# A gated attention/FFN decode step on one core: a wider row pitch for the heads' loads, a slice of w_gate by eight small transfers, and x and the gate vectors as rows

## The chip, the cores and the metric

The kernel runs on one core of a Trainium2 chip. The metric is the device time of one execution in microseconds (us); lower is better. The time before is 806.35 us, the median of three runs (806.04 to 806.44). A separate execution was profiled. Its page and its trace are what is read below.

The engines have these names in the profile: PE is the matrix engine (PEld its weight loads), DVE the vector engine, ACT the scalar engine, POOL the general-purpose engine, SP the engine that only issues transfers and waits. Transfers (DMAs) issued by SP or ACT are carried out by 16 DMA engines, which the profile sums up as one row.

## The reference

One token goes through two branches, which are mixed by a gate:

```python
g = sigmoid((x * gate_w).sum(-1))              # one number
a = attention(x) @ wo                          # 32 query heads, 4 kv heads, 65536 cached keys, head size 128
b = x + sigmoid(x @ w_r) * ((silu(x @ w_gate) * (x @ w_up)) @ w_down)   # d = 1024, f = 3584
out = g * a + (1 - g) * b                      # 1024 numbers
```

Everything is float32. With a single token the router's top-1 choice is that token, so the routing is the identity and only its sigmoid stays. The key and value caches have 4 x 65536 x 128 numbers each, 268 MB together; wq and wo are 33.6 MB, and the three FFN weights 44 MB. Each of these bytes is used once.

## The kernel before

**One stream of large loads.** All weights and caches were laid out anew on the host, so that the kernel reads them in one order. For each kv head `g` (G = 4) there are UNITS = 18 units of 32 KiB per partition: one of wq, eight of keys, eight of values, one of wo. Two units make one load, so a head has PER = 9 loads, and the array `heads` has 36 loads of 128 rows; a row is 2*CH = 16384 floats, 64 KiB, and goes to one partition. The rows of `heads` lie back to back. After them comes `ffn`, six loads of TAIL = 14336 floats (56 KiB) per partition: two for w_gate, two for w_up and two for w_down. The last two are cut into two and six pieces by `ENDS`, so that the last piece is small.

**Three buffers.** SP alone issues these loads (lines 114 to 127). Load `i` goes to buffer `i % 3`. From the fourth on, SP first waits for the mark of PE that frees the buffer (`LAST`, line 46): the mark that ends the second unit of the load three before. Two loads are thus issued or under way while PE works on a third.

**The work on a head.** PE forms q from x and wq (line 301), the scores per chunk of 8192 keys (line 317), and, after softmax, the values' sum (line 329) and the product with wo (line 346). ACT copies scores from PSUM and takes exponentials; DVE takes maxima and transposes. Only the gate values and q need x in other layouts: `xp` (line 93) is the stationary matrix for all products with x; column 0 of each of its eight 32-column blocks holds x, the other columns are zero.

**x and the gate vectors.** ACT issues two transfers at the start. `xk <- vecs` (line 149) brings x, gate_w and w_r as 128 rows of 96 bytes: partition p gets elements 8p to 8p+7 of each. `x_row <- x` (line 151) brings x once more, 256 floats to each of partitions 0, 32, 64 and 96. DVE copies xk into `xp` and forms the two dot products (lines 196 to 200). PE adds them up over the partitions (line 292), and q of head 0 follows. `x_row`, scaled by 1 - g, is the residual that is added at the end (lines 209, 269, 271).

**The FFN.** Line 373 multiplies x with w_gate and w_up: for each of eight row blocks `k` there are two banks `e` times four column groups `j` of FN = 448 columns, accumulated in PSUM. Group j writes partitions 32j to 32j+31. After `gate 1` ACT and DVE form the gated hidden vector, which is transposed on DVE and multiplied with w_down (lines 383 and 400). The last DVE instruction writes `fin` (line 271), and SP sends its rows 0, 32, 64, 96 to the output (line 129).

The order on each engine is the order of the lines; no scheduler moves anything. Engines wait for each other by semaphores: `marked` counts PE's marks, `ld0` to `ld2` and `end0` to `end7` the loads.

Of the kernel before, what the change touches and what calls it, by code (L numbers as in the profile page):

```python
# [8 lines left out]
P = 128  # L9
D = 1024  # L10
G = 4
HG = 8
DH = 128
SK = 65536
F = 3584
CH = 8192
# [3 lines left out]
KB = D // P  # L20
NQ = D // 4
FB = F // P
FN = F // 8
# [4 lines left out]
PER = UNITS // 2  # L28
BUFS = 3

TAIL = 14336
NTAIL = 3 * KB * F // TAIL

ENDS = {NTAIL - 2: [8 * D, TAIL], NTAIL - 1: [6 * D, 10 * D, 12 * D, 13 * D, 13 * D + 768, TAIL]}

PIECES = [(0, 192), (192, NQ)]

EARLY = 20

# [9 lines left out]
ACTED = {m: i + 1 for i, m in enumerate(ACTS)}  # L49


def gated_mix_kernel(nc, x, vecs, heads, ffn, out):

# [16 lines left out]
    pe, act, dve, pool, sp = nc.tensor, nc.scalar, nc.vector, nc.gpsimd, nc.sync  # L72

    stream = [nc.alloc_sbuf_tensor(f"st{b}", [P, 2 * CH], F32, align_bytes=256)[:, :] for b in range(BUFS)]
    scores = nc.alloc_sbuf_tensor("s", [P, NCH, 512], F32)[:, :, :]
# [3 lines left out]
    hp = scores[:, 2:4, :].rearrange("p a n -> p (a n)")[:, : FB * 32]  # L79
    att_sb = scores[:, 4, :]  # L80
    zeros = scores[:, 5, :]
    o_sb = scores[:, 0, :].rearrange("p (s d) -> p s d", s=4)

    def sb(name, *shape):
        t = nc.alloc_sbuf_tensor(name, [P, *shape], F32)
        return t[tuple(slice(None) for _ in range(len(shape) + 1))]

    xk = sb("xk", 3, KB)
    x_row, fin, q_sb = sb("x_row", NQ), sb("fin", NQ), sb("q_sb", 2 * NQ)
    ident, ones, md, lb = sb("ident", P), sb("ones", P), sb("md", P), sb("lb", P)  # L90
    sel, sel8, nsel, sel4 = sb("sel", 32), sb("sel8", HG), sb("nsel", HG), sb("sel4", 4)
    half, halves = sb("half", 2), sb("halves", 2, 32)
    xp, qp, op = sb("xp", KB, 32), sb("qp", 4, 32), sb("op", HG, 32)
# [3 lines left out]
    gate = sig[:, 0:1]  # L97
# [5 lines left out]
    ps_s = [ps_u[:, i, :] for i in range(2)]  # L103
    acc, ps_m, att, y = psum("acc", 512), psum("ps_m", P), psum("att", 512), psum("y", NQ)

    names = ["done", "fed", "x1", "x2", "acted", "pooled", "marked", "d2p", "d2a", "d2s", "self"]
    names += [f"ld{b}" for b in range(BUFS)] + [f"end{i}" for i in range(sum(map(len, ENDS.values())))]
    sems = {n: nc.alloc_semaphore(n) for n in names}
    nums = sorted(s.num for s in sems.values())
# [4 lines left out]
    for i in range(G * PER + NTAIL):  # L114
        b = i % BUFS
        if i >= BUFS:
            g, l = divmod(i - BUFS, PER)
            sp.wait_ge(sems["marked"], MARK[f"{LAST[l]} {g}" if g < G else ["gate 0", "gate 1", "up 0"][l]])
        if i < G * PER:
            sp.dma_start(stream[b], heads[i]).then_inc(sems[f"ld{b}"], 16)  # L120
        elif i - G * PER not in ENDS:
            sp.dma_start(stream[b][:, :TAIL], ffn[i - G * PER]).then_inc(sems[f"ld{b}"], 16)
        else:
            cuts = ENDS[i - G * PER]
            for c0, c1 in zip([0] + cuts, cuts):
                sp.dma_start(stream[b][:, c0:c1], ffn[i - G * PER, :, c0:c1]).then_inc(sems[f"end{len(ends)}"], 16)  # L126
                ends.append((i, c0, c1))
# [11 lines left out]
        out=ident, in_=ident, compare_op=ALU.not_equal, fill=1.0, base=0, pattern=[[-1, P]], channel_multiplier=1  # L139
# [3 lines left out]
    acted = []  # L143

    def tell(ins, name):
        acted.append(name)
        return ins.then_inc(sems["acted"])

    act.dma_start(xk, vecs).then_inc(sems["x1"], 16)
    act.wait_ge(sems["d2a"], 1)  # L150
    act.dma_start(
        x_row[::32, :], x.rearrange("(j n) -> j n", j=4)
    ).then_inc(sems["x2"], 16)
    act.wait_ge(sems["marked"], MARK["dot"])
    tell(act.activation(sig, ps_m[:, :2], AF.Exp, scale=-1.0), "sig")
    for g in range(G):
# [4 lines left out]
        for c in range(NCH):  # L161
            t = scores[:, c, :]
# [10 lines left out]
    def then(ins):  # L173

        own[0] += 1
        ins.then_inc(sems["self"])
        dve.wait_ge(sems["self"], own[0])
# [14 lines left out]
    dve.memset(qp, 0.0)  # L192
    dve.memset(zeros, 0.0)
    dve.memset(halves, 0.0)
    then(dve.memset(op, 0.0))
    dve.wait_ge(sems["x1"], 16)
    dve.tensor_copy(xp[:, :, 0], xk[:, 0, :])
    dve.tensor_mul(dots[:, 0, :], xk[:, 0, :], xk[:, 1, :])
    then(dve.tensor_mul(dots[:, 1, :], xk[:, 0, :], xk[:, 2, :]))
    to_pe(dve.tensor_reduce(dsum, dots, AX.X, ALU.add))  # L200
# [4 lines left out]

    then(dve.tensor_scalar(rest[:, 0:1], gate, -1.0, 1.0, op0=ALU.mult, op1=ALU.add))
    then(dve.tensor_mul(rest[:, 1:2], rest[:, 0:1], sig[:, 1:2]))
    dve.wait_ge(sems["x2"], 16)
    dve.tensor_scalar_mul(x_row, x_row, rest[:, 0:1])

    dve.wait_ge(sems["pooled"], 2)
# [64 lines left out]
    def mark(ins, name):  # L276
        marks.append(name)
        ins.then_inc(sems["marked"])

    def take(name, n=1):  # L280
        pe.wait_ge(sems[name], n).then_inc(sems[name], -n)  # L281
# [14 lines left out]
    with pe.Fori(0, G):  # L296
        loaded(0)
        for k in range(KB):
            for f in range(2):
                j = 2 * (k % 2) + f  # L300
# [23 lines left out]
        for c in range(NCH):  # L324
            loaded(1 + NCH + c)
            take("d2p")
            for m in range(NM):
                j = m % 4
# [3 lines left out]
                    stop=(c == NCH - 1 and m >= NM - 4),  # L332
# [10 lines left out]
        for h in range(HG):  # L343
            for f in range(2):
                j = 2 * (h % 2) + f
# [9 lines left out]
    def tail(first, n):  # L355
        i, c = divmod(first, TAIL)
        assert c + n <= TAIL
        if i < min(ENDS):
            if c == 0:
                take(f"ld{(G * PER + i) % BUFS}", 16)  # L360
        else:
            for e, (i1, c0, _) in enumerate(ends):
                if (i1 - G * PER, c0) == (i, c):
                    pe.wait_ge(sems[f"end{e}"], 16)
        return stream[(G * PER + i) % BUFS][:, c : c + n]


    for i, part in enumerate(("gate", "up")):
        ps = (ps_f, ps_u)[i]
        for k in range(KB):  # L370
            for e in range(2):
                for j in range(4):
                    ins = pe.matmul(  # L373
                        ps[32 * j : 32 * j + 32, e, :FN], xp[:, k, :], tail((i * KB + k) * F + (2 * j + e) * FN, FN),
                        start=(k == 0), stop=(k == KB - 1),
                    )
            if k % 4 == 3:
                mark(ins, f"{part} {k // 4}")
    take("d2p")
    for b in range(EARLY):  # L380
        for f in range(2):
            j = 2 * (b % 2) + f
            ins = pe.matmul(  # L383
                att[32 * j : 32 * j + 32, :], hp[:, 32 * b : 32 * b + 32], tail(2 * KB * F + b * D + f * 512, 512),
                start=(b < 2), stop=(b >= EARLY - 2),
            )
    mark(ins, "early")
    for b in range(EARLY, FB):
        if b == EARLY + 4:
            take("d2p")  # L390
            for j in range(4):
                ins = pe.matmul(
                    acc[32 * j : 32 * j + 32, :NQ], halves[:, j // 2, :], att_sb[:, j % 2 * NQ : (j % 2 + 1) * NQ],
                    start=True, stop=True,
                )
            mark(ins, "both")
        for c0, c1 in PIECES if b == FB - 1 else [(0, NQ)]:
            n = c1 - c0
            for j in range(4):
                ins = pe.matmul(  # L400
                    y[32 * j : 32 * j + 32, c0:c1], hp[:, 32 * b : 32 * b + 32], tail(2 * KB * F + b * D + 4 * c0 + j * n, n),
                    start=(b == EARLY), stop=(b == FB - 1 and c1 == NQ),
# [34 lines left out]
```

## Time and profile before

| what | value |
|---|---|
| median of three runs | 806.35 us (806.04 to 806.44) |
| profiled execution | 806.2 us |
| its span, first to last instruction | 804.8 us |
| PE busy | 399.5 us (50%) |
| DVE busy | 75.2 us (9%) |
| ACT busy | 44.5 us (6%) |
| bytes read | 346.05 MB, 430 GB/s over the span |
| granted PE clock | 0.758 |

The page shows the span in 40 slices with the busy share of each engine in tenths, and a row for the 16 DMA engines together. A table of DMA queues gives for each queue its packets, its megabytes and the time of its packets as a share of 16 engines' span: q1 is what SP issues, q10 what ACT issues, and q8 and q14 are fetches of instructions. The chain that ended last is followed back from the last instruction. The timeline lists instructions in order of time, with the idle time before each group in brackets. As PE starts on a load when it has landed, PE's starts in the timeline date the landings. A DMA query for a stretch of time gives the same queue table for that stretch alone; a packet counts in the stretch in which it starts, so shares of a short stretch can exceed 100%.

### The profile page before, as it was taken

How to read it: one execution, taken by the hardware profiler on the slowest of the kernel's cores; microseconds unless marked ns; L12 is line 12 of the kernel's file. 1: busy time of each engine (PE TensorE's matmuls, PEld its weight loads, DVE VectorE, ACT ScalarE, POOL GpSimd, SP SyncE). 2: the span in 40 equal slices, each digit the busy share in tenths (PEclk: the TensorE clock that was granted, in tenths of full speed). 3: DMA queues.
4: the chain of work that ended last, by engine and by line, in shares of the span. 5: the costliest groups of instructions: out<-in, count | busy, mean ns of one | idle time of the engine just before them, and what ended most of it. 6: DMA issues, size and time to landing. Idle time of an engine off the chain costs nothing. (4 is left out here: it accounts for less than half of the span.)

```text
span 804.8 us, 6104 instructions
## 1 busy us (share of the span) xinstructions
PE 399.5 (50%) x2810; PEld 119.5 (15%) x2810; DVE 75.2 (9%) x155; ACT 44.5 (6%) x99; POOL 0.7 (0%) x6
## 2 busy tenths in 40 slices
PE   0544463457554463445544454445444644564465
PEld 0211111112111121111111111111111111121121
DVE  0200010000000020000100110000000100000310
ACT  0000030000000030000000200000000300000000
POOL 0000000000000000000000000000000000000000
PEclk9976767767777786778777687687677677697679
DMA  9999999999999999999999999999999999999997
GB/s 417 417 418 466 414 423 460 417 428 453 420 430 453 420 430 450 423 430 450 423 430 446 427 430 446 427 431 443 427 433 443 427 433 443 421 442 428 436 416 335
DMA packets 7082, 346.20 MB, mean 430 GB/s; under 512 B 920, under 2 KB 1056, under 8 KB 1312
## 3 DMA queue, kind: packets, MB, share of 16 engines
q1 hardware_dynamic: 6920, 346.04, 99.4%
q8 instruction: 8, 0.13, 0.1%
q10 hardware_dynamic: 152, 0.02, 0.0%
q14 instruction: 2, 0.02, 0.0%
HBM read 346.05 MB, written 0.00 MB: 430 GB/s over the span
## 5 line engine op out<-in xcount | busy, mean ns | idle before, releaser
L317 PE MATMUL ps_u<-st,qp 128*32 128x512 f32 x1024 | 148.8, 743 | 154.7 <-PEq L281 154.7
L329 PE MATMUL acc<-st,pt 128*32 128x512 f32 x1024 | 149.9, 747 | 146.5 <-PEq L281 146.5
L317 PEld LDWEIGHTS ps_u<-st,qp 128*32 128x32 f32 x1024 | 40.8, 133 | 259.2 <-issue 259.2
L329 PEld LDWEIGHTS acc<-st,pt 128*32 128x32 f32 x1024 | 41.3, 133 | 251.9 <-issue 251.9
L159 ACT ACTIVATE s<-ps_u 128x512 f32<-128x512 f32 x32 | 19.1, 597 | 561.6 <-PE ps_u L317 561.6
L231 DVE TENSOR_REDUCE mx<-s 128x1 f32<-128x512 f32 x32 | 21.9, 686 | 285.3 <-ACT s L159 285.3
L246 DVE STREAM_TRANSPOSE pt<-s 128x512 f32<-128x512 f32 x32 | 22.7, 711 | 199.6 <-PE acc L329 196.1
L301 PE MATMUL ps_u<-st,xp 128*32 128x512 f32 x128 | 21.6, 835 | 19.8 <-PEq L281 19.8
L373 PE MATMUL ps_u<-st,xp 128*32 128x448 f32 x128 | 16.4, 678 | 17.5 <-PEq L281 17.5
L164 ACT ACTIVATE s<-s,nb 128x512 f32<-128x512 f32 x32 | 22.6, 708 | 10.5 <-DVE nb L241 10.5
L373 PE MATMUL ps_f<-st,xp 128*32 128x448 f32 x128 | 16.0, 664 | 14.1 <-PEq L281 14.1
L346 PE MATMUL att<-st,op 128*32 128x512 f32 x128 | 16.3, 653 | 2.4 <-PEq L281 2.4
L383 PE MATMUL att<-st,s 128*32 128x512 f32 x80 | 12.6, 782 | 7.8 <-DMA st<-in_ffn 5.3
L292 PE MATMUL ps_m<-dsum,ones 128*128 128x2 f32 x2 | 0.6, 348 | 23.6 <-PEq L281 23.6
L301 PEld LDWEIGHTS ps_u<-st,xp 128*32 128x32 f32 x128 | 5.7, 148 | 36.2 <-issue 36.2
L373 PEld LDWEIGHTS ps_u<-st,xp 128*32 128x32 f32 x128 | 5.2, 135 | 28.7 <-issue 28.7
L250 DVE COPY s<-acc 128x512 f32<-128x512 f32 x4 | 2.8, 691 | 70.0 <-PE acc L329 70.0
L373 PEld LDWEIGHTS ps_f<-st,xp 128*32 128x32 f32 x128 | 5.5, 131 | 24.7 <-issue 24.7
L221 DVE COPY q_sb<-ps_u 128x512 f32<-128x512 f32 x4 | 2.8, 691 | 51.6 <-PE ps_u L301 51.6
L167 ACT ACTIVATE s<-ps_f 128x896 f32<-128x896 f32 x1 | 0.9, 917 | 103.7 <-PE ps_f L373 103.7
L346 PEld LDWEIGHTS att<-st,op 128*32 128x32 f32 x128 | 4.9, 118 | 10.4 <-issue 10.4
L323 PE MATMUL ps_m<-md,ones 128*128 128x128 f32 x8 | 2.0, 328 | 8.2 <-PEq L281 8.2
(65 smaller groups left out, 66.9 us busy)
## 6 DMA issues: line engine op xcount, KB each, us to landing
st<-in_ffn SPq DMA_DIRECT2D x4, 7168.0 KB, 42.8
st<-in_ffn SPq DMA_DIRECT2D x2, 3072.0 KB, 37.5
st<-in_ffn SPq DMA_DIRECT2D x1, 4096.0 KB, 35.2
st<-in_ffn SPq DMA_DIRECT2D x1, 2048.0 KB, 37.2
st<-in_ffn SPq DMA_DIRECT2D x1, 1024.0 KB, 39.2
st<-in_heads SPq DMA_DIRECT2D x36, 48.1
st<-in_ffn SPq DMA_DIRECT2D x1, 512.0 KB, 40.0
st<-in_ffn SPq DMA_DIRECT2D x1, 384.0 KB, 40.5
```

Source lines behind the costliest of these rows:

```text
L159: tell(act.activation(scores[:, c, :], ps_s[c % 2], AF.Copy), f"s{c} {g}")
L164: act.activation(t, t, AF.Exp, bias=nb, scale=SCALE, accum_out=sums[:, c : c + 1]), f"e{c} {g}"
L221: to_pe(dve.tensor_copy(q_sb, ps_s[0]))
L231: ins = dve.tensor_reduce(mx[:, c : c + 1], scores[:, c, :], AX.X, ALU.max)
L246: to_pe(dve.transpose(pts[:, c % 2, :], scores[:, c, :]))
L250: to_pe(dve.tensor_copy(o_sb, acc.rearrange("p (s d) -> p s d", s=4)))
L301: ins = pe.matmul(ps_s[0][32 * j : 32 * j + 32, :], xp[:, k, :], unit(0)[:, k * D + f * 512 : k * D + (f + 1) * 512], start=(k < 2), stop= ...
L317: ins = pe.matmul(ps_s[c % 2][32 * j : 32 * j + 32, :], qp[:, s, :], unit(1 + c)[:, (4 * s + j) * 512 : (4 * s + j + 1) * 512], start=(s = ...
L329: ins = pe.matmul(acc[32 * j : 32 * j + 32, :], pts[:, c % 2, 32 * m : 32 * m + 32], unit(1 + NCH + c)[:, m * 512 : (m + 1) * 512], start= ...
L346: ins = pe.matmul(att[32 * j : 32 * j + 32, :], op[:, h, :], unit(UNITS - 1)[:, h * D + f * 512 : h * D + (f + 1) * 512], start=False, sto ...
L373: ins = pe.matmul(ps[32 * j : 32 * j + 32, e, :FN], xp[:, k, :], tail((i * KB + k) * F + (2 * j + e) * FN, FN), start=(k == 0), stop=(k == ...
L383: ins = pe.matmul(att[32 * j : 32 * j + 32, :], hp[:, 32 * b : 32 * b + 32], tail(2 * KB * F + b * D + f * 512, 512), start=(b < 2), stop= ...
```

## The change

The change has three parts.

- **Pitch.** In memory, the rows of `heads` are now PITCH = 17408 floats (68 KiB) apart in place of 64 KiB. A load still brings the first 64 KiB of each row, and the 4 KiB behind it are never read.
- **Side.** The last 256 of the columns of w_gate in row block k = 3 no longer come with the first load of `ffn`, whose rows are 1 KiB shorter on all 128 partitions. They come as an array `side` of 32 rows of 4 KiB, to partitions 0 to 31, by eight transfers of four rows each. SP issues one of them after each of loads 0, 3, 6 up to 21. PE multiplies them by four matmuls of 32 rows and 256 columns, with x from `xside` in `xs`, after row block 4 of the gate; the matmul that read these columns before is narrower by 256.
- **x as rows.** x, gate_w and w_r come as 12 rows of 1 KiB, by three transfers of four rows, into partitions i, 32+i, 64+i, 96+i of `x_row`. A DVE transpose makes `xk` of it. A fourth transfer, `xside`, brings the part of x that goes with `side` (32 rows of 16 bytes). All four are issued by ACT, after DVE has cleared `x_row`. DVE waits once for all of them. The order of x over partitions and blocks has changed with this, and so has the host's layout of wq, w_gate and w_up.

Some small tiles (`fin`, `q_sb`, `lb` and `xk`) now lie inside `scores` in place of tiles of their own.

```diff
+PITCH = 2 * CH + 1024
+SIDE = 256
...
+    fin = scores[:, 7, :NQ]
+    q_sb, lb = scores[:, 1, :], scores[:, 2, :P]
-    xk = sb("xk", 3, KB)
+    xs_sb = sb("xs_sb", 4)[:32]
+    xt = scores[:, 6, :NQ]
+    xk = xt.rearrange("p (k q) -> p q k", q=32)
+    side_sb, xs = sb("side", 4, SIDE)[:32], sb("xs", 4, 32)[:32]
...
-            sp.dma_start(stream[b], heads[i]).then_inc(sems[f"ld{b}"], 16)
+            sp.dma_start(stream[b], heads[i, :, : 2 * CH]).then_inc(sems[f"ld{b}"], 16)
+            if i % 3 == 0 and i // 3 < 8:
+                rows = slice(i // 12 * 16 + i // 3 % 4, i // 12 * 16 + i // 3 % 4 + 13, 4)
+                sp.dma_start(side_sb[rows], side[rows]).then_inc(sems["side"], 16)
         elif i - G * PER not in ENDS:
-            sp.dma_start(stream[b][:, :TAIL], ffn[i - G * PER]).then_inc(sems[f"ld{b}"], 16)
+            n = TAIL - SIDE * (i == G * PER)
+            sp.dma_start(stream[b][:, :n], ffn[i - G * PER, :, :n]).then_inc(sems[f"ld{b}"], 16)
...
-    act.dma_start(xk, vecs).then_inc(sems["x1"], 16)
     act.wait_ge(sems["d2a"], 1)
-    act.dma_start(
-        x_row[::32, :], x.rearrange("(j n) -> j n", j=4)
-    ).then_inc(sems["x2"], 16)
+    for i in range(3):
+        act.dma_start(x_row[i::32, :], vecs[i].rearrange("(j n) -> j n", j=4)).then_inc(sems["x"], 16)
+    act.dma_start(xs_sb, xside).then_inc(sems["x"], 16)
...
+    dve.memset(xs, 0.0)
     then(dve.memset(op, 0.0))
-    dve.wait_ge(sems["x1"], 16)
+    dve.wait_ge(sems["x"], 64)
+    then(dve.transpose(xt, x_row))
     dve.tensor_copy(xp[:, :, 0], xk[:, 0, :])
+    dve.tensor_copy(xs[:, :, 0], xs_sb)
...
-    dve.wait_ge(sems["x2"], 16)
...
+                    n = FN - SIDE * ((part, k, e, j) == ("gate", 3, 1, 3))
                     ins = pe.matmul(
-                        ps[32 * j : 32 * j + 32, e, :FN], xp[:, k, :], tail((i * KB + k) * F + (2 * j + e) * FN, FN),
+                        ps[32 * j : 32 * j + 32, e, :n], xp[:, k, :], tail((i * KB + k) * F + (2 * j + e) * FN, n),
                         start=(k == 0), stop=(k == KB - 1),
                     )
+            if (part, k) == ("gate", 4):
+                pe.wait_ge(sems["side"], 128)
+                for m in range(4):
+                    pe.matmul(
+                        ps[96:128, 1, FN - SIDE : FN], xs[:, m, :], side_sb[:, m, :], start=False, stop=False,
+                        tile_position=(0, 96),
+                    )
...
+    heads = np.zeros((G, PER, P, PITCH), np.float32)
+    heads[..., : 2 * CH] = np.concatenate([wq, k, v, wo], axis=2).reshape(G, P, PER, 2 * CH).transpose(0, 2, 1, 3)
...
+        "vecs": np.stack([a[n].reshape(D) for n in ("A_x", "gate_w", "B_w_r")]),
+        "xside": a["A_x"].reshape(4, KB, 32)[:, 3].T,
+        "side": gate_up[0][:, :, 3, F - SIDE :].transpose(1, 0, 2),
+        "heads": heads.reshape(G * PER, P, PITCH),
```

More of the change, by code (lines that the diff above doesn't have):

```diff
@@ L49, with gated_mix_kernel @@
 ACTED = {m: i + 1 for i, m in enumerate(ACTS)}
-def gated_mix_kernel(nc, x, vecs, heads, ffn, out):
+def gated_mix_kernel(nc, vecs, xside, side, heads, ffn, out):
     pe, act, dve, pool, sp = nc.tensor, nc.scalar, nc.vector, nc.gpsimd, nc.sync
@@ L86, in sb @@
         return t[tuple(slice(None) for _ in range(len(shape) + 1))]
-    xk = sb("xk", 3, KB)
-    x_row, fin, q_sb = sb("x_row", NQ), sb("fin", NQ), sb("q_sb", 2 * NQ)
-    ident, ones, md, lb = sb("ident", P), sb("ones", P), sb("md", P), sb("lb", P)
+    xs_sb = sb("xs_sb", 4)[:32]
+    xt = scores[:, 6, :NQ]
+    xk = xt.rearrange("p (k q) -> p q k", q=32)
+    side_sb, xs = sb("side", 4, SIDE)[:32], sb("xs", 4, 32)[:32]
+    x_row, ident, ones, md = sb("x_row", NQ), sb("ident", P), sb("ones", P), sb("md", P)
     sel, sel8, nsel, sel4 = sb("sel", 32), sb("sel8", HG), sb("nsel", HG), sb("sel4", 4)
@@ L104, in gated_mix_kernel @@
     acc, ps_m, att, y = psum("acc", 512), psum("ps_m", P), psum("att", 512), psum("y", NQ)
-    names = ["done", "fed", "x1", "x2", "acted", "pooled", "marked", "d2p", "d2a", "d2s", "self"]
+    names = ["done", "fed", "x", "acted", "pooled", "marked", "d2p", "d2a", "d2s", "self", "side"]
     names += [f"ld{b}" for b in range(BUFS)] + [f"end{i}" for i in range(sum(map(len, ENDS.values())))]
@@ L413 @@
     a = {n: np.asarray(t) for n, t in inputs.items()}
-    wq = a["A_wq"].reshape(P, KB, G, HG * DH).transpose(2, 0, 1, 3).reshape(G, P, -1)
+    wq = a["A_wq"].reshape(4, KB, 32, G, HG * DH).transpose(3, 0, 2, 1, 4).reshape(G, P, -1)
     wo = a["A_wo"].reshape(G, HG, P, D).transpose(0, 2, 1, 3).reshape(G, P, -1)
@@ L418 @@
     v = a["A_v_cache"].reshape(G, NCH, P, NB, DH).transpose(0, 2, 1, 3, 4).reshape(G, P, -1)
-    heads = np.concatenate([wq, k, v, wo], axis=2).reshape(G, P, PER, 2 * CH).transpose(0, 2, 1, 3)
+    heads = np.zeros((G, PER, P, PITCH), np.float32)
+    heads[..., : 2 * CH] = np.concatenate([wq, k, v, wo], axis=2).reshape(G, P, PER, 2 * CH).transpose(0, 2, 1, 3)
     down = a["B_w_down"].reshape(4, FB, 32, D).transpose(0, 2, 1, 3).reshape(P, FB, D).copy()
@@ L422 @@
     down[:, -1] = np.concatenate([last[:, :, c0:c1].reshape(P, -1) for c0, c1 in PIECES], axis=1)
-    ffn = np.concatenate([t.reshape(P, -1) for t in (a["B_w_gate"], a["B_w_up"], down)], axis=1)
+    gate_up = [a[n].reshape(4, KB, 32, F).transpose(0, 2, 1, 3) for n in ("B_w_gate", "B_w_up")]
+    ffn = np.concatenate([t.reshape(P, -1) for t in gate_up + [down]], axis=1)
     arrays = {
-        "x": a["A_x"].reshape(D),
-        "vecs": np.stack([a[n].reshape(P, KB) for n in ("A_x", "gate_w", "B_w_r")], axis=1),
-        "heads": heads.reshape(G * PER, P, 2 * CH),
+        "vecs": np.stack([a[n].reshape(D) for n in ("A_x", "gate_w", "B_w_r")]),
+        "xside": a["A_x"].reshape(4, KB, 32)[:, 3].T,
+        "side": gate_up[0][:, :, 3, F - SIDE :].transpose(1, 0, 2),
+        "heads": heads.reshape(G * PER, P, PITCH),
         "ffn": ffn.reshape(P, NTAIL, TAIL).transpose(1, 0, 2),
```

## The prediction

> **What bounds the kernel now.** I read the page's slices and queue table first, then the chain that ended last, then PE's timeline for the landing of each load, then SP's waits, then the queue table for short stretches. The page:
>
> ```profile
> span 804.8 us, 6104 instructions
> DMA  9999999999999999999999999999999999999997
> q1 hardware_dynamic: 6920, 346.04, 99.4%
> q8 instruction: 8, 0.13, 0.1%
> q10 hardware_dynamic: 152, 0.02, 0.0%
> ```
>
> The 16 DMA engines are busy from the first slice to the last, and 99.4% of their time is SP's own loads. From the q1 row follows a price: 0.994 x 804.8 us x 16 engines over 346.04 MB is 37.0 us per MB of one engine, that is 37.9 ns for 1 KiB. The chain that ended last (start, length, what):
>
> ```profile
> 761.19 40.50 DMA st<-in_ffn
> ...
> 801.74 0.69 PE y L400 x16
> ...
> 802.52 0.48 DVE fin L271
> ```
>
> It ends in the last load; behind its landing at 801.69 (761.19 + 40.50) lie only some 3 us of PE, DVE and the output. The profiled execution took 806.2 us, 1.4 more than its span, and lies 0.15 under the median of 806.35; the sum below is made against 806.2. PE's timeline (start, length, ..., idle time before):
>
> ```profile
> 25.84 4.73 PE L301 MATMUL ps_u<-st,xp 128*32 128x512 f32 x32
> ...
> 42.13 8.55 PE L317 MATMUL ps_u<-st,qp 128*32 128x512 f32 x64 [5.33 <-PEq L281]
> 63.10 10.00 PE L317 MATMUL ps_u<-st,qp 128*32 128x512 f32 x64 [12.42 <-PEq L281]
> 82.41 8.89 PE L317 MATMUL ps_u<-st,qp 128*32 128x512 f32 x64 [9.30 <-PEq L281]
> 101.72 6.04 PE L317 MATMUL ps_u<-st,qp 128*32 128x512 f32 x32 [10.42 <-PEq L281]
> ...
> 700.57 5.29 PE L329 MATMUL acc<-st,pt 128*32 128x512 f32 x32 [9.46 <-PEq L281]
> ...
> 717.33 7.92 PE L373 MATMUL ps_f<-st,xp 128*32 128x448 f32 x64 [5.08 <-PEq L281]
> 734.29 8.07 PE L373 MATMUL ps_f<-st,xp 128*32 128x448 f32 x64 [9.04 <-PEq L281]
> 751.18 8.15 PE L373 MATMUL ps_u<-st,xp 128*32 128x448 f32 x64 [8.82 <-PEq L281]
> 768.06 8.25 PE L373 MATMUL ps_u<-st,xp 128*32 128x448 f32 x64 [8.72 <-PEq L281]
> ```
>
> These starts date the landings. From the third load (63.10) to the 36th (700.57) lie 33 loads of 8 MiB in 637.47 us, 19.317 us each, 434.3 GB/s. The FFN's loads of 7 MiB take 16.91 (717.33 to 768.06, three) or 16.885 (the last two); scaled by 8/7 that is 19.33 or 19.30. The idle times of 5 to 12 us show that PE has room in each period. So does SP:
>
> ```profile
> SPq L120 <- PE ps_u L317: 305.5, 16, 34.8
> ...
> SPq L126 <- PE ps_f L373: 16.8, 1, 16.8
> ```
>
> SP waits for buffers while two loads are queued, so a later release costs nothing until it eats that queue.
>
> **One thing is uneven: instruction fetches.** The interval from 42.13 to 63.10 is 20.97 us, 1.65 above the period. In 45 to 48 us:
>
> ```profile
> q8 instruction: 1, 0.02, 1.9%
> ```
>
> One fetch took 1.9% of 16 x 3 us, 0.91 us, of one engine, and what it delays makes that engine some 1.65 late; each load waits for its slowest engine. The page has eight fetches, yet the period later stays at 19.31 to 19.32, so no other fetch hit the same engine. The end shows it too. The stretch 799.5 to 801.8, in 40 slices:
>
> ```profile
> DMA  9398797995970929191817373532626344231000
> ...
> q1 hardware_dynamic: 283, 0.52, 58.2%
> q8 instruction: 1, 0.02, 2.5%
> ```
>
> Some engines end over 1 us before others. 39.3% of 2.3 us, 0.90 us, is idle on average, so perfect balance would save at most 0.9.
>
> **The change part by part.**
>
> *Side.* Each of the 16 engines loses 8 rows x 1 KiB, 8 x 37.9 ns = 0.30 us. The eight transfers bring the same 128 KiB back. Which engines carry them? The output's transfer has four rows too, and the queue table of its stretch (803.5 to 805) reads:
>
> ```profile
> DMA packets 8, 0.00 MB, mean 3 GB/s; under 512 B 4, under 2 KB 8, under 8 KB 8
> ```
>
> That is four rows and four counts, so four engines; the 48 large loads leave 16 counts each (6144 rows + 48 x 16 + 8 = 6920). If the eight transfers rotate over the engines, each gets two rows: +0.30, in sum nothing. If it is always the same four, these get 32 KiB, 1.21 us, and eight counts of about 0.01 each, so net +0.99, and the twelve others -0.30. [...]
>
> What that does to the end depends on whether these four carry a fetch. A fetch makes an engine 1.65 late; the shift is 0.99 + 0.30 = 1.29, less than that. If none of the four has a fetch, the fetch-laden engines still end last, 0.30 earlier. If one has, it ends 0.99 later than the latest now. So the bounds are -0.30 and +0.99. If seven fetches before the end fell at random, the four would be free in 7% of cases; if they step from engine to neighbouring engine, which would be one way never to hit one twice, six of 16 starting places leave four neighbours free. I take -0.30, though it is a narrow choice: it is the value for which the late engines' own row (20.97) decides, and the fetches do seem to keep apart. The +0.99 is the first rival.
>
> SP issues the eight transfers between loads, at the 0.33 us that a load's issue takes; the 305.5 us of SP's waits cover them. The four added matmuls are narrower than line 400's:
>
> ```profile
> L400 PE MATMUL y<-st,s x72: 219/379/403, 797.1 to 802.2; 128*32 128x256 f32 x56, 128*32 128x192 f32 x8, 128*32 128x64 f32 x8
> L246 DVE STREAM_TRANSPOSE pt<-s 128x512 f32<-128x512 f32 x32 | 22.7, 711 | 199.6 <-PE acc L329 196.1
> ```
>
> or as wide: 4 x 0.40 = 1.6 us, before `gate 1`. Behind them PE idles 8.82 us ahead of the load at 751.18, and SP, which waits for `gate 1` on line 126, has that load and the next queued. Their wait for `side` is on transfers issued some 500 us before. Cost zero; without that cover it would be 1.6.
>
> *Pitch.* The same rows of 64 KiB are read, so no byte is saved. What it can give is bounded by the period: 36 x (19.317 - 19.297) = 0.7 us by the best FFN rate, -0.3 by the other. The FFN's rows lie 56 KiB apart and run no slower, so a pitch that is not a power of two does no harm there. I take -0.2, the middle, with 0 to -0.7 kept as bounds, and harm as a rival. [...]
>
> *x as rows.* In 20 to 24 us the queue table has:
>
> ```profile
> q10 hardware_dynamic: 32, 0.00, 0.5%
> ```
>
> 32 small packets in 0.32 us, 10 ns each. Nine of them leave each engine and three (two rows of xside, a count) come; the four engines get two more rows of 1 KiB, 0.08, and two counts. That is -0.06 on twelve engines and about +0.04 on four. I take -0.05. The wait at the start moves:
>
> ```profile
> 22.98 0.17 DVE L197 COPY xp<-xk 128x8 f32<-128x8 f32 x1 [20.41 <-DMA xk<-in_vecs]
> ...
> 27.40 0.35 DVE L209 TENSOR_SCALAR x_row<-x_row,rest 128x256 f32<-128x256 f32 x1 [2.20 <-DMA x_row<-in_x]
> ...
> 36.85 0.60 ACT L159 ACTIVATE s<-ps_u 128x512 f32<-128x512 f32 x1 [12.44 <-PE ps_u L317]
> ```
>
> xk's nine packets per engine landed 22 us after issue, and x_row's two behind them 4.4 later: a small packet and a large one seem to take turns. The new queue has at most nine on an engine (three rows, their counts, two rows, one count), so x lands between 23 and 27.4. The transpose of 128x256 adds half of 711 ns, the new memset and copy some 0.3. PE's first chunk then ends by 41 in place of 36.8, where SP waits for `s0` to issue the fourth load; two loads are queued until 63.10, so 20 us of cover remain. Nothing waits on ACT's longer issue but `sig`. Cost zero.
>
> The aliases inside `scores` move no wait on the path: `fin` is written after its area's last use, `q_sb` and `lb` in the order of DVE and PE as before.
>
> *Sum.* 806.2 - 0.30 - 0.20 - 0.05 = 805.65, and with the 0.15 to the median 805.8.
>
> **The rivals.**
>
> *A fetch on one of the four engines.* The end moves by +0.99 + 0.04 - 0.2: 807.2, inside what can be told from no change. For it: half of the engines have a fetch. Against it: fetches that step in neighbours can miss four.
>
> *The pad slows the heads' rows* (the other side). Rows at 68 KiB may meet in the memory where rows at 64 KiB do not. It decides from 1.6 us, 0.23% of 36 x 19.317 = 695.4 us. The rates of two stretches differ by that much already:
>
> ```profile
> 400.00:600.00 200.00, 96.02 (x672) 28.13 (x664) 16.77 (x34) 12.31 (x27) 0.00 (x0) 0.75 1.00 435
> 600.00:700.00 100.00, 49.57 (x322) 13.54 (x322) 9.13 (x18) 7.54 (x19) 0.00 (x0) 0.72 1.00 433
> ```
>
> 435 against 433 GB/s is 0.46%, though a stretch's edges alone can make it; over the heads it is 3.2 us, 809.3 with the rest. Against it: the 56 KiB rows.
>
> [...]
>
> *The side transfers rotate*, so that nothing is balanced: 806.1. It stays within the forecast's class.
>
> **How the numbers follow.** About 0.2% (1.6 us, 804.74 to 807.96) is what a measurement of this kernel can tell from no change. Forecast 0.42, a fetch on the four 0.29, rotation 0.03: same 0.74. The pad slows 0.13; the pad mends the start 0.13. Range: the forecast's own is 805.2 (0.7 for the pad, nothing left) to 806.2; with the first rival's upper end, 806.35 + 1.03 = 807.4, and a little of the start's gain, 804.7 to 807.5 leaves out less than 2 in 10.
>
> **What would show it.** Right: the period of the heads' loads stays 19.30 to 19.32, the interval with the first fetch stays near 21, and the last landing comes 0.3 to 0.6 earlier against the first packets. The tail's slices then fall off more steeply. A last landing 0.7 to 1.0 later with the same period is the fetch rival. A period of 19.36 or more would show the pad slowing rows; a second load earlier than 41.5 the start mended. x should be in use by 28 us, and PE's idle time before 751 be 1.6 shorter. The prediction fails if the added small transfers cost their engine more than their bytes, or if fetches move.

## The result, and the profile after

The changed kernel takes 812.42 us in the median of eleven runs, against 806.21 for the kernel before in eleven runs beside it. The ratio is 1.0084 (95% interval 1.0066 to 1.0102), 6.2 us by the medians. Ratios here and below leave out runs more than 1.5% above the fastest of their kernel, such as the one at 819.08, or two of the kernel before at 1183 and 1869 us in later rounds, while medians and ranges are of all runs. The spread is new. Before, all eleven runs lie between 806.04 and 806.44; after, they lie between 806.90 and 819.08, and they cluster: one at 806.9, five at 812.3 to 812.4, three at 814.1 to 814.2, two at 819. The profiled execution took 814.1, with a span of 812.5.

The page's slices and queue table of the changed kernel:

```profile
span 812.5 us, 6132 instructions
DMA  9999999999999999999999999999999999999997
GB/s 410 417 443 433 417 458 418 442 424 433 445 426 414 390 384 394 436 439 423 442 426 430 448 423 445 423 436 440 429 448 413 439 439 432 428 447 421 436 421 332
q1 hardware_dynamic: 6984, 346.04, 99.4%
```

The DMA row is as full as before and the queue's share is the same 99.4%. What changed is the row beneath it: in slices 14 to 16 the engines move 384 to 394 GB/s while they count as fully busy. The packets take longer. PE's timeline dates it:

```profile
237.34 9.81 PE L336 MATMUL ps_u<-st,qp 128*32 128x512 f32 x64 [10.18 <-PEq L300]
256.75 8.65 PE L336 MATMUL ps_u<-st,qp 128*32 128x512 f32 x64 [9.60 <-PEq L300]
278.46 6.30 PE L336 MATMUL ps_u<-st,qp 128*32 128x512 f32 x32 [13.05 <-PEq L300]
...
300.08 8.77 PE L348 MATMUL acc<-st,pt 128*32 128x512 f32 x64 [4.57 <-PEq L300]
321.85 8.53 PE L348 MATMUL acc<-st,pt 128*32 128x512 f32 x64 [13.00 <-PEq L300]
341.16 9.11 PE L348 MATMUL acc<-st,pt 128*32 128x512 f32 x64 [10.78 <-PEq L300]
```

The load that PE starts on at 256.75 took its normal 19.4 us. The three behind it took 21.71, 21.62 and 21.77, and the next 19.31 again. Three loads lose 7.2 us together, and 814.1 - 7.2 = 806.9 is the time of the fastest run. Counted from 0, these are loads 13, 14 and 15. SP issued side transfers after loads 12 and 15: the slow stretch begins with the load behind one of them and ends with the load behind the next. The rate in stages (the last column):

```profile
200.00:240.00 40.00, 20.51 (x148) 6.42 (x144) 3.14 (x8) 1.79 (x3) 0.00 (x0) 0.71 1.01 439
255.00:310.00 55.00, 29.97 (x194) 8.61 (x194) 6.68 (x13) 7.54 (x19) 0.00 (x0) 0.74 1.00 386
340.00:400.00 60.00, 32.44 (x214) 10.21 (x218) 3.88 (x12) 0.60 (x1) 0.00 (x0) 0.76 1.00 434
400.00:600.00 200.00, 100.81 (x705) 29.79 (x701) 16.51 (x34) 12.32 (x27) 0.00 (x0) 0.77 1.00 435
```

386 against 435 GB/s is 11% less at a DMA share of 1.00 (the number before it). PE's granted clock, 0.74 in the stretch beside 0.71 to 0.77 outside, doesn't set it apart. In the trace all packets of 64 KiB that start between 260 and 315 us take 2.67 us or more, where the kernel before has 2.42 in the median: all 16 engines are slower, not four. Outside the stretch the 68 KiB rows of `heads` run at 434 to 439 GB/s in this table, the rate of the 64 KiB rows before (434.3).

### The profile page after: what moved, and what is told of

It reads as the page before. It is cut to its first block, busy times and chain, and to the rows that moved or that the text cites. A ratio compares the mean times of both kernels' runs of the same rounds, so it can differ in the third digit from the quotient of the medians.

```text
span 812.5 us, 6132 instructions
## 1 busy us (share of the span) xinstructions
PE 397.6 (49%) x2818; PEld 120.0 (15%) x2818; DVE 75.9 (9%) x158; ACT 44.5 (5%) x99; POOL 0.7 (0%) x6
## 3 DMA queue, kind: packets, MB, share of 16 engines
q1 hardware_dynamic: 6984, 346.04, 99.4%
## 5 line engine op out<-in xcount | busy, mean ns | idle before, releaser
L348 PE MATMUL acc<-st,pt 128*32 128x512 f32 x1024 | 147.4, 737 | 158.2 <-PEq L300 158.2
L348 PEld LDWEIGHTS acc<-st,pt 128*32 128x32 f32 x1024 | 43.1, 132 | 259.4 <-issue 256.6
L365 PE MATMUL att<-st,op 128*32 128x512 f32 x128 | 20.7, 803 | 2.4 <-PEq L300 2.4
L393 PE MATMUL ps_f<-st,xp 128*32 128x448 f32 (+1 forms) x128 | 14.0, 583 | 12.9 <-PEq L300 12.9
L240 DVE COPY s<-ps_u 128x512 f32<-128x512 f32 x4 | 2.8, 692 | 50.3 <-PE ps_u L320 50.3
L181 ACT ACTIVATION_READ_ACCUMULATOR s<-s,nb 128x1 f32 x32 | 6.0, 187 | 0.0
```

Of the source, the lines that this page charges most:

```text
L181: act.activation(t, t, AF.Exp, bias=nb, scale=SCALE, accum_out=sums[:, c : c + 1]), f"e{c} {g}"
L240: to_pe(dve.tensor_copy(q_sb, ps_s[0]))
L348: ins = pe.matmul(acc[32 * j : 32 * j + 32, :], pts[:, c % 2, 32 * m : 32 * m + 32], unit(1 + NCH + c)[:, m * 512 : (m + 1) * 512], start= ...
L365: ins = pe.matmul(att[32 * j : 32 * j + 32, :], op[:, h, :], unit(UNITS - 1)[:, h * D + f * 512 : h * D + (f + 1) * 512], start=False, sto ...
L393: ins = pe.matmul(ps[32 * j : 32 * j + 32, e, :n], xp[:, k, :], tail((i * KB + k) * F + (2 * j + e) * FN, n), start=(k == 0), stop=(k == K ...
```

## The experiments

Three theories stood first. P: rows 68 KiB apart meet in the memory. S: the side transfers alone start the slow stretches. B: it takes both. Each kernel was run beside the kernel before (806.2 to 806.5 in the medians).

**One part at a time.** e1 is the kernel before with the new pitch alone:

```diff
-            sp.dma_start(stream[b], heads[i]).then_inc(sems[f"ld{b}"], 16)
+            sp.dma_start(stream[b], heads[i, :, : 2 * CH]).then_inc(sems[f"ld{b}"], 16)
```

(with the padded array on the host, as in the change).

> The kernel before with one edit: rows of heads 68 KiB apart. In the changed kernel three loads in a row (14th to 16th) take 21.7 us in place of 19.31, 2.4 us each, 7.2 in all. Theory P (the pitch alone makes rows meet in the memory): some runs 5 to 13 us above the kernel before, and in the profile some loads at about 21.7. Theory S (the side transfers alone do it): 805.5 to 806.5, all loads at 19.3. Theory B (it takes both, the pitch and engines that were put out of step by the side transfers): as S, 805.5 to 806.5.

Measured: 806.25 (806.11 to 806.61), ratio 0.9998 (0.9988 to 1.0008). P falls: the pitch alone costs and gives nothing that shows.

e2 is the changed kernel with the old pitch:

```diff
-PITCH = 2 * CH + 1024
+PITCH = 2 * CH
```

> The changed kernel with one edit: rows of heads 64 KiB apart again; side transfers and x as rows stay. Theory P: no slow loads, 806 to 807.3 (the side transfers' own -0.3 to +1.0). Theory S: some loads at 21.7, runs of 811 to 819. Theory B: as P, no slow loads, 806 to 807.3.

Measured: 814.22, with runs from 806.83 to 825.20. The stretches come without the pitch, so S holds and B falls. The profiled execution even has its stretch in the same place:

```profile
256.29 9.75 PE L336 MATMUL ps_u<-st,qp 128*32 128x512 f32 x64 [10.19 <-PEq L300]
278.16 5.62 PE L336 MATMUL ps_u<-st,qp 128*32 128x512 f32 x32 [12.12 <-PEq L300]
...
299.80 8.48 PE L348 MATMUL acc<-st,pt 128*32 128x512 f32 x64 [5.71 <-PEq L300]
321.57 9.54 PE L348 MATMUL acc<-st,pt 128*32 128x512 f32 x64 [13.29 <-PEq L300]
341.05 4.49 PE L348 MATMUL acc<-st,pt 128*32 128x512 f32 x20 [9.95 <-PEq L300]
```

e3 is the changed kernel without the side transfers:

```diff
-            if i % 3 == 0 and i // 3 < 8:
-                rows = slice(i // 12 * 16 + i // 3 % 4, i // 12 * 16 + i // 3 % 4 + 13, 4)
-                sp.dma_start(side_sb[rows], side[rows]).then_inc(sems["side"], 16)
```

(also the narrow matmul and the four added ones.)

> The changed kernel without the side transfers: the first load of ffn brings all columns again, and the four added matmuls are gone; 68 KiB pitch and x as rows stay. Theory P: some loads at 21.7, runs of 811 to 819. Theory S and theory B: no slow loads, 805.5 to 806.5.

Measured: 806.51 (806.16 to 806.73), ratio 1.0001 (0.9992 to 1.0011). Pitch and x as rows together are neutral. All the loss is the side transfers'.

**What about a side transfer starts a stretch?** A packet of 4 KiB takes 0.16 us in the trace, so four of them on four engines don't by themselves fill the other engines' time for 65 us. Three new theories. W: the stretches come from a transfer whose engines write partitions that other engines write in the loads. T: each transfer pushes its four engines 0.16 us out of step. Q: the loads issued behind a small transfer are handled in another way. Which engine writes which partition the profile doesn't show. For W I assumed that the last four side transfers, to partitions 16 to 31, are of this kind, and that transfers to 32 to 47 would not be. All partitions but 0 to 15 and 32 to 47 are called foreign below, by their place alone. From here on the pitch is 64 KiB.

e4 moves the last four transfers to partitions 32 to 47 (x for them and their products are split in two groups to match):

```diff
-                sp.dma_start(side_sb[rows], side[rows]).then_inc(sems["side"], 16)
+                to = slice(rows.start + i // 12 * 16, rows.stop + i // 12 * 16, 4)
+                sp.dma_start(side_sb[to], side[rows]).then_inc(sems["side"], 16)
```

> The changed kernel at a pitch of 64 KiB, with one more edit: the last four side transfers write partitions 32 to 47 in place of 16 to 31 (same bytes, same four rows each, same times; eight matmuls of 16 rows in place of four of 32). [...] Theory W (the slow stretches come from engines that write partitions which belong to other engines): no loads at 21.7, 805.9 to 807.3. Theory T (the four engines are pushed out of step by 0.16 us at each transfer, and slow stretches come at certain offsets): as with the partitions 16 to 31, several runs at 811 to 825. Theory Q (the loads issued behind a small transfer on SP's queue are handled in another way): as theory T.

Measured: 807.40, all ten runs within 807.21 to 807.68; ratio 1.0012 (1.0002 to 1.0021). The stretches are gone with the same rows read, the same bytes, times and offsets, which fits W and speaks against T and Q.

e5 puts partitions 16 to 31 first:

```diff
-                rows = slice(i // 12 * 16 + i // 3 % 4, i // 12 * 16 + i // 3 % 4 + 13, 4)
+                r0 = (1 - i // 12) * 16 + i // 3 % 4
+                rows = slice(r0, r0 + 13, 4)
```

> The changed kernel at a pitch of 64 KiB, with the two halves of the side transfers in the other order: partitions 16 to 31 after loads 0, 3, 6, 9, partitions 0 to 15 after loads 12, 15, 18, 21. Theory W: the slow loads now lie among loads 1 to 12, and none follows load 15. Theory T: the offsets grow as before, so slow loads begin with load 13 as before. Theory Q: no prediction of the place; slow loads wherever.

Measured: 859.49 in four runs, from 809.80 to 901.80. The stages of the profiled one:

```profile
22.00:80.00 58.00, 30.30 (x210) 9.22 (x210) 7.66 (x27) 3.16 (x6) 0.00 (x0) 0.79 1.01 389
80.00:220.00 140.00, 57.00 (x396) 16.58 (x396) 10.21 (x21) 7.54 (x19) 0.00 (x0) 0.72 1.00 376
...
400.00:600.00 200.00, 94.72 (x622) 27.68 (x614) 15.51 (x33) 10.52 (x24) 0.00 (x0) 0.71 1.01 388
610.00:700.00 90.00, 44.84 (x298) 13.11 (x298) 7.64 (x18) 5.30 (x9) 0.00 (x0) 0.73 0.99 431
```

The stretch now starts with the second load, behind the first transfer to partitions 16 to 31, as W had it and T had not. W's other half was wrong: none of the transfers to partitions 0 to 15 ended it, and it ran to about 605 us, far beyond load 15. The three further transfers to partitions 16 to 31, after loads 3, 6 and 9, didn't end it either. In 602 to 606 us the queue table has one fetch of instructions, and the normal rate returns at that time:

```profile
q8 instruction: 1, 0.02, 1.6%
```

e7 issues the same transfers from ACT:

```diff
+            if g < 2 and c % 2 == 0:
+                rows = slice(g * 16 + c // 2, g * 16 + c // 2 + 13, 4)
+                act.dma_start(side_sb[rows], side[rows]).then_inc(sems["side"], 16)
```

> The changed kernel at a pitch of 64 KiB, with the eight side transfers issued by ACT in place of SP, four in head 0 (partitions 0 to 15) and four in head 1 (16 to 31). Theory W: slow stretches in head 1 as before, some runs at 811 to 825. Theory T: also slow stretches, as the offsets are the same. Theory Q: none, 806 to 807.3.

Measured: 818.65, from 807.40 to 920.00. The profiled execution, at 809.7, has one slow load of 22.14 us in head 1:

```profile
217.98 9.23 PE L336 MATMUL ps_u<-st,qp 128*32 128x512 f32 x64 [8.24 <-PEq L300]
240.12 8.41 PE L336 MATMUL ps_u<-st,qp 128*32 128x512 f32 x64 [12.91 <-PEq L300]
259.76 2.79 PE L336 MATMUL ps_u<-st,qp 128*32 128x512 f32 x12 [11.23 <-PEq L300]
```

Q falls: transfers from another queue start them as well.

e6 issues all eight behind each other after load 12:

```diff
-            if i % 3 == 0 and i // 3 < 8:
+            if i == 12:
+                for n in range(8):
+                    rows = slice(n // 4 * 16 + n % 4, n // 4 * 16 + n % 4 + 13, 4)
```

> The changed kernel at a pitch of 64 KiB, with all eight side transfers issued one behind the other after load 12. In the profiles so far a slow stretch began with the load behind one side transfer and ended with the load behind the next. Theory W: the stretch can begin with load 13, and with no side transfer behind it, it can last for many loads, 2.4 us each, up to 23 x 2.4 = 55 us (runs up to 861), or, if the last of the eight ends it, not at all (806 to 807.3). Theory T: one fixed offset of 8 x 0.16 us, so either no slow load or all 23 of them. Theory Q: one stretch of loads at most, three or so, 806 to 814.

Measured: 807.55 (807.35 to 807.93). No stretch in ten runs. That is W's second branch, so it doesn't test W. But it shows that a foreign transfer doesn't start a lasting stretch each time: four in a row left none.

**One transfer, by place, size and width.** All of these build on e4, which has no stretches, and add transfers whose data nobody reads. e8 adds one after load 12:

```diff
+            if i == 12:
+                sp.dma_start(side_all[16:29:4], side[0:13:4]).then_inc(sems["side"], 16)
```

> The kernel in which all side transfers write partitions 0 to 15 and 32 to 47 (807.4 us), with one transfer more, after load 12: four rows of 4 KiB to partitions 16, 20, 24, 28 of a place that nobody reads. Theory W: this one transfer is enough; a slow stretch begins with load 13 in most runs, 7 us or more (814 and up). A theory N, by which it takes several such transfers or the partitions of the whole series, expects 807.3 to 807.8 as without it.

Measured: 813.03 in four runs (812.66 to 873.49). One transfer of 16 KiB to foreign partitions is enough; the rows that it reads are ones that the first side transfers read too. Its profile:

```profile
256.49 9.43 PE L343 MATMUL ps_u<-st,qp 128*32 128x512 f32 x64 [10.48 <-PEq L307]
279.39 6.49 PE L343 MATMUL ps_u<-st,qp 128*32 128x512 f32 x32 [13.47 <-PEq L307]
...
300.91 9.41 PE L355 MATMUL acc<-st,pt 128*32 128x512 f32 x64 [4.17 <-PEq L307]
320.22 9.99 PE L355 MATMUL acc<-st,pt 128*32 128x512 f32 x64 [9.90 <-PEq L307]
```

Two loads lose 3.6 and 2.2 us, then the period is 19.31 again. In 293 to 297 us lies a fetch, near the stretch's end:

```profile
q14 instruction: 1, 0.01, 0.6%
```

This 5.8 us is about the step from 806.9 to the changed kernel's cluster at 812.4. That a fetch ended the stretch there too wasn't profiled.

e11 goes to partitions 64, 68, 72, 76 (`side_all[64:77:4]` in the line above).

> As e8, with the one added transfer to partitions 64, 68, 72, 76 in place of 16, 20, 24, 28. Theory W: a slow stretch as in e8, 814 and up in most runs. If it is something about partitions 16 to 31 alone: 807.3 to 807.8.

Measured: 870.59, from 807.45 to 913.48. In the profiled execution the stretch began at load 13 and still ran in the FFN's loads:

```profile
100.00:250.00 150.00, 80.83 (x532) 23.66 (x532) 13.36 (x29) 9.33 (x22) 0.00 (x0) 0.72 1.00 433
260.00:300.00 40.00, 16.78 (x118) 4.54 (x110) 5.25 (x11) 7.54 (x19) 0.00 (x0) 0.76 1.01 392
400.00:600.00 200.00, 87.03 (x596) 25.50 (x596) 14.78 (x32) 10.53 (x24) 0.00 (x0) 0.71 1.00 387
...
730.00:780.00 50.00, 25.10 (x170) 8.08 (x174) 2.86 (x7) 0.00 (x0) 0.00 (x0) 0.70 1.00 385
```

It is not partitions 16 to 31 that matter, and not the pitch of `heads`: the FFN's rows slow down too. The stretch ends near 836 us, and there the queue table of 835 to 838 us has a fetch:

```profile
790.00:834.00 44.00, 23.29 (x160) 7.22 (x164) 7.47 (x3) 0.92 (x1) 0.00 (x0) 0.73 0.99 383
838.00:862.00 24.00, 15.18 (x105) 3.69 (x101) 2.77 (x3) 0.00 (x0) 0.00 (x0) 0.79 0.98 421
```

```profile
q8 instruction: 1, 0.02, 2.3%
```

Three fetches before it, near 293, 378 and 804 us, ended nothing.

e10 sends rows of 1 KiB, four times:

```diff
+            if i in (12, 15, 18, 21):
+                r0 = 16 + i // 3 - 4
+                sp.dma_start(side_all[r0 : r0 + 13 : 4, 0], side[r0 : r0 + 13 : 4, 0]).then_inc(sems["side"], 16)
```

> As e8, but after each of loads 12, 15, 18 and 21 four rows of only 1 KiB go to partitions 16 to 31. Theory W as it stands says nothing on size: slow stretches as with 4 KiB. If the two writers must overlap for long enough (0.04 us in place of 0.16), fewer or none: 807.3 to 807.8. [...]

Measured: 807.49 (807.28 to 807.70), no stretch. e14 is the same with rows of 2 KiB (`:2` in place of `0`).

> As e10, with rows of 2 KiB in place of 1 KiB, four transfers of four rows to partitions 16 to 31. If the length of the overlap decides (0.04 us at 1 KiB: no stretch in ten runs; 0.16 us at 4 KiB: a stretch in nearly all), some runs at 812 and up, the others at 807.4 to 807.8. If 4 KiB is needed: all at 807.4 to 807.8.

Measured: 877.74 in four runs, from 859.45 to 890.14, each 50 us or more above e4. So the bound lies between 1 and 2 KiB here, but longer rows aren't worse: four such transfers of 4 KiB in e2 gave 806.83 to 825.20. In the profile the first three did nothing lasting. The stretch began behind the fourth, near 429 us, and is deeper:

```profile
260.00:400.00 140.00, 75.27 (x516) 22.45 (x508) 12.66 (x28) 8.73 (x21) 0.00 (x0) 0.75 1.00 433
450.00:600.00 150.00, 70.03 (x468) 20.74 (x468) 11.29 (x26) 7.54 (x19) 0.00 (x0) 0.71 1.00 366
...
600.00:763.00 163.00, 67.69 (x452) 19.31 (x448) 12.27 (x24) 9.33 (x22) 0.00 (x0) 0.70 1.00 367
766.00:800.00 34.00, 19.90 (x144) 6.64 (x144) 0.37 (x2) 0.92 (x1) 0.00 (x0) 0.80 0.99 429
```

No foreign transfer came behind the fourth. The end lies in 763 to 766 us, and again a fetch lies there (764.7).

e9 adds one transfer of 32 rows of 4 KiB, `side_all[64:96]`.

> As the last, but the added transfer after load 12 brings 32 rows of 4 KiB to partitions 64 to 95 at once. [...] Theory W: slow stretches here too, 814 and up in many runs. If only transfers on four engines do it: 807.5 to 808.2 (8 KiB more for each engine, 0.3 us).

Measured: 808.45 (808.26 to 808.83), no stretch in eight runs; 1.05 above e4, or 1.3 with each set against the kernel before beside it, where its bytes explain 0.3. e13 adds four such transfers, two of 32 and two of 16 rows.

> As the kernel with one added transfer of 32 rows, but with four added transfers, after loads 12, 15, 18, 21: 32 rows to partitions 64 to 95, 32 to 96 to 127, 16 to 16 to 31, 16 to 48 to 63. Theory W4 (slow stretches need a transfer on a few engines, so that most engines run against a few): 808.0 to 809.5, no stretch. Theory W (any writer of a foreign partition can start one): with four chances, some runs at 812 and up.

Measured: 811.38 in four runs (811.11 to 811.93), 4.0 above e4 where the bytes explain 0.9 (two times 0.3 and two times half of it). These transfers too cost more than their bytes, but once for each; nothing lasts. W in its general form falls for these widths. e15 sends eight rows, `side_all[64:93:4]`.

> As e11, with eight rows of 4 KiB in one transfer to partitions 64, 68, up to 92, after load 12, so on eight engines. Theory W and theory W4: slow stretches, many runs at 812 and up. If it takes just four engines: 807.4 to 808.0.

Measured: 807.56, but one of ten runs at 864.36. That run was not profiled. As none of the kernel before's 92 runs in these rounds lies between 807.2 and 1183, it was probably a stretch; if so, eight engines start one far more rarely than four. The packet counts bear out the widths: against e4's 6984, e8 has 8 more (four rows, four counts), e15 16 (eight and eight) and e9 48 (32 and 16).

**The terms of the sum.** e12 has no side transfers but keeps the shorter first load of `ffn`:

```diff
+            n = TAIL - SIDE * (i == G * PER)
+            sp.dma_start(stream[b][:, :n], ffn[i - G * PER, :, :n]).then_inc(sems[f"ld{b}"], 16)
```

> The changed kernel at a pitch of 64 KiB without any side transfer, and with the first ffn load short by 1 KiB a row as in the change: the last 256 columns of row block 3 of w_gate are left out of the product. This is the term -0.30 of the prediction by itself: 805.8 to 806.1. Against the kernel with all side transfers on partitions 0 to 15 and 32 to 47 (807.4) it gives what 32 KiB on each of four engines cost: 1.3 to 1.6, if one of the four was among the last to end (the prediction's first rival).

Measured: 806.04 (805.74 to 806.41) beside 806.40 for the kernel before, 0.36 less, though the ratio's interval (0.9986 to 1.0005) doesn't exclude nothing. The last piece's landing, in the chains of e12 and then of e4 (start, length, what):

```profile
761.57 39.81 DMA st<-in_ffn
```

```profile
761.79 40.59 DMA st<-in_ffn
```

801.38 against 802.38: the side transfers on partitions 0 to 15 and 32 to 47 move the end by 1.0 in these two profiles and by 1.4 in the medians. The DMA slices of e4's last stretch (801.0 to 803.3) show a few engines working on alone:

```profile
DMA  1956767643211020201110100000000000000000
...
q1 hardware_dynamic: 134, 0.16, 19.1%
```

No version that beats the kernel before came out of this: pitch and x as rows change nothing, and the side transfers lose even on partitions 0 to 15 and 32 to 47.

## Why the prediction was wrong

The prediction was 805.8 us, no change that can be measured, with a range to 807.5. The measured 812.42 lies outside. By its steps; the last ones rest on these rows of the changed kernel, of its timeline (PE's second load, its first FFN load for `up`, the new transpose) and of the view of the tile `side`:

```profile
42.54 9.94 PE L336 MATMUL ps_u<-st,qp 128*32 128x512 f32 x64 [5.61 <-PEq L300]
...
758.89 7.61 PE L393 MATMUL ps_u<-st,xp 128*32 128x448 f32 x64 [7.41 <-PEq L300]
```

```profile
22.91 0.45 DVE L215 STREAM_TRANSPOSE s<-x_row 128x256 f32<-128x256 f32 x1 [20.21 <-DMA xs_sb<-in_xside]
```

```profile
L137 SPq DMA_DIRECT2D side<-in_side x8: 599/599/729, 1.2 to 391.5; - x8
...
L400 PE MATMUL ps_f<-side,xs x8: 374/374/398, 744.9 to 746.5; 32*32 32x256 f32 x8
```

- **Side, the bytes: the bounds were right.** -0.30 for the shorter rows measured -0.36 (e12), within noise of nothing. With e4, four engines with 32 KiB more end 0.9 above the kernel before, and 1.4 above e12 (1.3 with each set against the kernel before beside it) where 1.29 was worked out. The queue table confirms four engines: 6984 packets are the 6920 of before and eight times four rows and four counts.
- **Side, the choice: wrong.** Between -0.30 and +0.99 I took the lower, on the hope that none of the four engines carries a fetch. e4 is the first rival as priced: 807.4 where 807.2 was given, or 807.4 without the 0.2 that it took for the pad. Its own working (7% at random, six of 16 in a row) had spoken for the rival. That the four engines are the same each time, which both bounds take, no run showed then; e4's 1.3 to 1.4 above e12 fits it, where transfers that rotate would have given 0.3. That a fetch is what made one of the four late isn't shown.
- **Side, what was left out: the step that failed.** The sum charged the added transfers to the engines that carry them, by bytes, and nothing to the others. A transfer of four rows of 4 KiB to partitions 16 to 31 (e5, e8) or 64 to 76 (e11) slowed all loads, down to 376-392 GB/s in the stages of e5 and e11, beside 434, for 40 us (e8) up to 580 (e11). It costs between nothing and some 100 us from run to run, 6 us in the median for the change. "The added small transfers cost their engine more than their bytes" stood among the things that would make the prediction fail, but with no price and no chance.
- **Pitch: right, near zero.** e1 gives 0.9998 where -0.2 us was taken. The comparison of the loads' periods was the right reading: nothing at 64 KiB was slow (434.3 GB/s, beside 434.7 for the FFN's rows at 56 KiB), so there was nothing to mend. The rival on the other side ended with a time near the measured one (809.3; its terms add up to 809.2) for a reason that e1 excludes.
- **The start: not mended.** PE starts on the second load at 42.54, not before 41.5; before it was 42.13. The 0.13 for a mended start and the start's gain in the range count on up to 1.8 us: in the kernel before the first packets come about 1.7 us into the span (slice 12 of 40 in the row below, of its first 6 us), and two loads of 19.3 us from there would land at 40.3. No run shows that the pitch has a part in these 1.8 us, and e1, with the pitch alone, gained nothing.

```profile
DMA  0000000000099990000000000000000099999000
```

- **x as rows: right, no cost.** x is there at 22.91, just before the 23 to 27.4 given; the transpose takes 0.45 where 0.36 was estimated. e3 holds it together with the pitch at 1.0001.
- **Matmuls and issue: right, hidden.** SP takes 0.60 us for a side transfer where 0.33 was taken, and its waits cover it. PE spends 744.9 to 746.5 on the added products, and its idle time before `up` falls from 8.82 to 7.41.

## What to carry to other kernels

When 16 engines stream at full rate (434 GB/s here), a small transfer isn't priced by its bytes alone. If it runs on a few engines, try it on several partitions: here 0 to 15 with 32 to 47 gave no stretch (e4), while 16 to 31 and 64 to 76 gave some (e8, e11). Or spread it over all of them, which cost 1 us or so for each transfer here but started no stretch (e9, e13); and look at the spread of several runs, since one of the changed kernel's eleven runs, at 806.9, showed next to nothing of the loss. A full DMA row is no proof of full rate: read the GB/s beside the share (386 at a share of 1.00 here).

## What the runs showed of the hardware

- A single transfer of four rows of 2 or 4 KiB to foreign partitions (16 to 31 in e5, e8 and e14, 64 to 76 in e11) lowered the rate of all engines together from 433-435 to 366-392 GB/s, and the lower rate outlived the transfer by tens to hundreds of microseconds (e5, e8, e11, e14). Not each such transfer did it: in the changed kernel's profile the first of four did, in e14's only the fourth.
- In the profiles the lower rate ended at another such transfer (the changed kernel, e2, e7) or within a few microseconds of a fetch of instructions (e5, e8, e11, e14). That the fetch ends it is argued from its place in time alone. Not each of them did: e5's stretch goes on behind three more such transfers, and e11's runs past three fetches.
- With rows of 1 KiB (ten runs), or transfers of 16 and 32 rows of 4 KiB (twelve runs of e9 and e13; e9's 32 rows leave 16 counts), no stretch came; with eight rows on eight engines, one run of ten was as long as one with a stretch.
- What the engines do in a stretch isn't visible in the profile: they count as busy, and each packet takes longer (2.67 us or more for 64 KiB, beside 2.42). Why it starts, and why it goes on after the last foreign write, is left open.
